# A fused retention and ELU feed-forward kernel: one weight part issued earlier, two FFN1 tiles in other PSUM banks, one weight transfer in place of two, and two units placed later

## The chip, the cores and the metric

The kernel runs on one core of a Trainium2 chip. Its time is the device time of an execution in microseconds (us), as the median of several runs. One execution was profiled; its trace has the start and the duration of each instruction on the engines: PE (TensorE, the matmuls, with PEld for its weight loads), DVE (VectorE), ACT (ScalarE), POOL (GpSimd) and SP (SyncE, which only issues transfers here). All places in time below are microseconds from the start of the profiled span.

## The reference

Retention (attention without softmax, with a decay by distance for each head) is followed by a feed-forward layer with an ELU between its two matmuls:

```python
batch, n_heads, seq, head_dim = (8, 8, 576, 64)      # q, k, v; float32
scores = (1 / sqrt(D)) * q @ k^T
gamma = 1 - 2 ** (-5 - arange(H))
Dmat = where(rel >= 0, gamma ** rel, 0)              # rel = row - column
attn = (scores * Dmat) @ v
x = attn.transpose(0, 2, 1, 3).reshape(4608, 512)
h = x @ w_in                                         # w_in 512 x 2048
g = where(h > 0, h, exp(min(h, 0)) - 1)
out = g @ w_out                                      # w_out 2048 x 512; float32
```

## The kernel before

**Units and groups.** The 4608 rows are cut into 36 units of 128 rows. Units come in groups (`GROUPS`): the first has units 0 to 2, then units 3, 4 and 5 stand alone, then groups of two, three and at last four units. A group's FFN1 has 16 tiles of 128 hidden columns; each tile is four matmuls over 128 x (128 times the group's units). `f1(g, n)` takes as many tiles at once as fill 512 columns of a bank: one for a group of three or four units, two for a group of two, four for a group of one.

**A unit's retention.** `scale_v` (POOL, L172) scales v by a decay factor for each key. `turn` (L180) transposes q and k on PE into a score tile in PSUM, and DVE copies one half out, then ACT the other (units from 12 on are transposed by a transfer instead). `scores` (L203) puts the products of keys and queries in PSUM, `masks` (DVE, L216) applies the causal mask, `inter` and `intra` (L227, L267) add what the carried state and the unit's own keys give, `state` and `state_out` (L243, L260) update the carried state, and `put_x` (DVE, L279) applies the decay for each query and writes the columns of `xt`, the input of FFN1. `product(u)` is `inter`, `state`, `intra`, `put_x` and `state_out` in a row. `stretch(u)` (L289) does the same for unit u, with the scores and masks of unit u + 1 around it.

**FFN1 and ELU.** `ffn1` (L336) issues the matmuls of a tile (`ph`), ACT takes the exponential (`e`, L354), POOL makes `m = e - 1` (L356), and DVE makes `g = min(max(ph, 0), m)` (L316), which is the ELU, since `m` is positive only where `ph` is. DVE's part is queued later than the others: `late` holds it until `tick` has been called three times (L318), and `finish(n)` (L312) queues what is n ticks old. `ffn1_part` (L324) issues the matmuls of a tile for some units only; `f1` then does the rest. `ffn2` and `ffn2_half` multiply g by w_out.

**PSUM.** FFN1 tiles use three `ps_h` banks (`h`) in turn and, where a tile is given the bank `m`, the single `ps_m` bank. The pool `ps_s` holds one tile of two banks, used by `turn` and `scores` one after the other. A bank is free for the next tile when its last reader is done; for an FFN1 tile this is DVE's g.

**The order of the work.** It is written out by hand up to FFN1 of group 2 (L419 to L512). In the first FFN1, tiles 0 to 3 are begun for units 0 and 1, `product(2)` is put between, and then all 16 tiles follow, with unit 3 among them: its turn after tile 5, its scores and `scale_v(3)` after tile 7, its product after tile 10. FFN1 of unit 3 follows, then halves of FFN2 of units 0 to 3. From there on a planner orders the work (L515 to L572): `slots` is the list of FFN1 and FFN2 pieces of PE, each of length about 1; `due` gives each unit a place in slots, interpolated between the starts of groups; `events` place the stretch of unit u at `due[u]`, `scale_v` of unit u + 2 at the same place, and the turn of unit u + 2 at a share of the way to the next unit. An event is queued ahead of the first slot whose middle lies at or past its place.

**Transfers.** POOL's queue issues the q and k loads and the weights, since these are cast to bf16 on the way. Weights come in parts: `load_w_in(n)` is a quarter of w_in, which serves tiles 4n to 4n + 3, and `load_w_out(c, f0, f1)` a piece of the column half c of w_out. v goes through SP's queue, except for unit 3. `load_v` with a second argument first lets that engine write one element of the buffer, which holds the transfer back until that engine gets there. POOL is in order: an issue stands in the same queue as `m` and `scale_v`.

Of the kernel before, what the change touches and what calls it, by code (L numbers as in the profile page):

```python
# [9 lines left out]
FP32 = mybir.dt.float32  # L10
BF16 = mybir.dt.bfloat16
I32 = mybir.dt.int32
AF = mybir.ActivationFunctionType
ALU = mybir.AluOpType
# [3 lines left out]
def kernel(  # L18
# [12 lines left out]
    B, H, S, D = q.shape  # L31
    DM, DF = moe_w_in.shape
    P = 128
    HP = H // 2
# [3 lines left out]
    R = 2 * S // P  # L38
# [9 lines left out]
    def place(u):  # L48

        pair, r = divmod(u, R)  # L50
        if r < 4:
            return [(0, 2 * pair, P * r, P)]
        if r == 4:
            return [(0, 2 * pair, 4 * P, 64), (64, 2 * pair + 1, 0, 64)]
        return [(0, 2 * pair + 1, 64 + P * (r - 5), P)]
# [6 lines left out]
    nat = ctx.enter_context(tc.tile_pool(name="nat", bufs=5))  # L62
# [9 lines left out]
    ps_s = ctx.enter_context(tc.tile_pool(name="ps_s", bufs=1, space=PSUM))  # L72
# [4 lines left out]
    raws, kns = {}, {}  # L77
# [10 lines left out]
    def load_qk(u, *cs):  # L88

        if u not in kns:  # L90
            kns[u] = qkpool.tile([P, 2, H, D], BF16, name="qkn", tag="qkn")
        for c in cs or (0, 1):
            for p0, b, s0, n in place(u):
                nc.gpsimd.dma_start(  # L94
                    kns[u][p0 : p0 + n, c], (q, k)[c][b, :, s0 : s0 + n, :].rearrange("h p d -> p h d")
                )
# [6 lines left out]
    def load_w_in(n):  # L103
        s = slice(n * 512, (n + 1) * 512)
        nc.gpsimd.dma_start(w_in_sb[:, :, s], w_in_v[:, :, s])

    def load_w_out(c, f0, f1):
        s = (slice(None), slice(f0, f1), slice(c * 256, c * 256 + 256))
        nc.gpsimd.dma_start(w_out_sb[s], w_out_v[s])
# [51 lines left out]
    gk = const.tile([P, R, H], FP32, name="gk")  # L161
# [7 lines left out]

    qkTs, vns, scs, pts, os_, sbs, sts = {}, {}, {}, {}, {}, {}, {}  # L170

    def scale_v(u):  # L172
        rv = raws[u]
        n = nat.tile([P, H, D], BF16, name="vn", tag="vn")
        nc.gpsimd.tensor_tensor(  # L175
            n, rv, gk[:, u % R].unsqueeze(2).to_broadcast([P, H, D]), ALU.mult
        )
        vns[u] = n

    def turn(u, bank=None, keys_on_v=False):  # L180

# [21 lines left out]
    def scores(u):  # L203
        t = qkTs[u]
        sc = ps_s.tile([P, 2, HP, P], FP32, name="sc", tag="sc")
        for hp in range(HP):
            for j in range(2):
                for i in range(2):
                    r = slice(i * D, (i + 1) * D)
                    nc.tensor.matmul(  # L210
                        sc[j * 64 : (j + 1) * 64, i, hp], t[r, 1, hp, j * 64 : (j + 1) * 64], t[r, 0, hp],
                        start=(hp == 0), stop=(hp == HP - 1), skip_group_check=True,
                    )
        scs[u] = sc

    def masks(u, i=None):  # L216

        if u not in pts:
            pts[u] = ppool.tile([P, 2, HP, P], BF16, name="pt", tag="pt")
        m = mask[:, 1 if u % R == 4 else 0]  # L220
        s = slice(0, 2) if i is None else slice(i, i + 1)
        nc.vector.tensor_tensor(  # L222
            pts[u][:, s].rearrange("p i h t -> p (i h) t"), scs[u][:, s].rearrange("p i h t -> p (i h) t"),
            m.unsqueeze(1).to_broadcast([P, (s.stop - s.start) * HP, P]), ALU.mult,
        )

    def inter(u):  # L227

        o = ps_o.tile([P, HP, P], FP32, name="o", tag="o")
        os_[u] = o  # L230
        r = u % R
        if r == 0:
            return
        n = 64 if r == 4 else P
        for hp in range(HP):
            for i in range(2):
                rows = slice(i * D, (i + 1) * D)
                nc.tensor.matmul(  # L238
                    o[rows, hp, :n], sbs[u][rows, hp], qkTs[u][rows, 0, hp, :n],
                    start=(hp == 0), stop=False, skip_group_check=True,  # L240
                )

    def state(u):  # L243

        r = u % R
        if r == 8:
            return
        if r in (0, 4):
            sts[0] = ps_st.tile([P, HP, D], FP32, name="st", tag="st")
        st = sts[0]  # L250
        rows = slice(64, P) if r == 4 else slice(0, P)
        for hp in range(HP):
            for i in range(2):
                h = 2 * hp + i
                nc.tensor.matmul(  # L255
                    st[i * D : (i + 1) * D, hp], kns[u][rows, 1, h], vns[u][rows, h],
                    start=(hp == 0 and r in (0, 4)), stop=(r in (3, 7)), skip_group_check=True,
                )
# [8 lines left out]
    def intra(u):  # L267
        o = os_[u]
        for hp in range(HP):
            for i in range(2):  # L270
                h = 2 * hp + i
                nc.tensor.matmul(  # L272
                    o[i * D : (i + 1) * D, hp], vns[u][:, h], pts[u][:, i, hp],
                    start=(u % R == 0 and hp == 0), stop=(hp == HP - 1), skip_group_check=True,
                )
# [3 lines left out]
    def put_x(u):  # L279
        g, i = group_of[u]  # L280
        if i == 0:
            xts[g] = xpool.tile([P, KJ, 512], BF16, name="xt", tag="xt")
        r = u % R
        s0 = P * r if r < 5 else 64 + P * (r - 5)
        nc.vector.tensor_tensor(  # L285
            xts[g][:, :, i * P : (i + 1) * P], os_[u], gx[:, :, s0 : s0 + P], ALU.mult
        )

    def stretch(u, ahead=True):  # L289

        ahead = ahead and u + 1 < NU
        if ahead:
            scores(u + 1)
        inter(u)
        state(u)
        intra(u)
        last = GROUPS[group_of[u][0]][-1] == u
        if last:
            put_x(u)
        if ahead:  # L300
            masks(u + 1)
        if not last:
            put_x(u)
        state_out(u)
# [7 lines left out]
    def finish(n=0):  # L312

        while late and late[0][0] <= slot[0] - n:
            _, gt_, ph, m, _ = late.pop(0)
            nc.vector.scalar_tensor_tensor(gt_, ph, 0.0, m, ALU.max, ALU.min)  # L316
# [5 lines left out]
    phs = {}  # L322

    def ffn1_part(g, ft, u0, u1, bank=None):  # L324

        pool, tag = bank or (ps_h, "ph")
        if (g, ft) not in phs:
            phs[g, ft] = pool.tile([P, 512], FP32, name="ph", tag=tag)
        c = slice(u0 * P, u1 * P)
        for j in range(KJ):  # L330
            nc.tensor.matmul(  # L331
                phs[g, ft][:, c], w_in_sb[:, j, ft * P : (ft + 1) * P], xts[g][:, j, c],
                start=(j == 0), stop=(j == KJ - 1), skip_group_check=True,
            )
# [74 lines left out]
    def product(u):  # L409
        inter(u)  # L410
        state(u)
        intra(u)
        put_x(u)
        state_out(u)

    h, m = (ps_h, "ph"), (ps_m, "pm")
# [7 lines left out]
    scale_v(0)  # L424
    load_w_in(1)
    scale_v(1)
    load_qk(3)
    load_v(3, queue=nc.gpsimd)
    scale_v(2)
    load_w_in(2)  # L430
    load_w_in(3)
    load_w_out(0, 0, 8)
    load_w_out(0, 8, 16)
    load_w_out(1, 0, 16)
    dummy(2)
    for u in range(2):
# [13 lines left out]
    def f1(g, n, bank=None):  # L450
        k = 512 // (P * len(GROUPS[g]))
        ffn1(g, k * n, bank)
# [4 lines left out]
    product(2)  # L457
    for n in range(2, 4):
        ffn1_part(0, n, 0, 2, m if n == 3 else None)
    for n in range(4):  # L460
        ffn1_part(0, n, 2, 3)
        f1(0, n)
    for n in range(4, 16):
        f1(0, n, m if n % 4 == 3 else None)
        if n == 5:
            turn(3)
        if n == 7:
            scores(3)
            masks(3, 0)
            scale_v(3)  # L470
        if n == 8:
            masks(3, 1)
        if n == 10:
            product(3)
    for n in range(4):
        f1(1, n, m if n == 3 else None)
        if n == 0:
            load_v(4, nc.vector)
        if n == 1:
            load_qk(4)  # L480
    finish()
    load_qk(5)
    load_v(5, nc.vector)
# [32 lines left out]
    for g in range(3, NG + 1):  # L516
# [10 lines left out]
        while a < len(f1s) or b < len(f2s):  # L527
# [4 lines left out]
                slots.append(f1s[a])  # L532
                a += 1
            now += slots[-1][3]
    due = {5: 0.0}
    last = 5
    for g in range(4, NG):
        u1 = GROUPS[g][-1]
# [3 lines left out]
    events = []  # L542
    for u in range(5, NU):
        def at(share):
            return due[u] + share * (due[u + 1] - due[u])
        events.append((due[u], 0, u))
        if u + 2 < PE_TURNED:
            events += [(due[u], 3, u + 2), (at(0.5), 1, u + 2)]
        if PE_TURNED <= u + 3 < NU:
            t = at(0.4) if u + 2 < PE_TURNED else due[u]  # L550
            events += [(t, 1, u + 3), (t, 3, u + 3)]
        if u + 5 < NU:
            events += [(at(0.25), 4, u + 5), (at(0.6), 5, u + 5)]
# [3 lines left out]
    for f, g, s, d in slots:  # L557
        while events and events[0][0] <= now + d / 2:
            _, kind, u = events.pop(0)
# [13 lines left out]
    u = NU - 1  # L573
# [31 lines left out]
```

## Time and profile before

| | us |
|---|---|
| median of 5 runs | 316.66 (316.49 to 317.78) |
| the profiled execution | 317.78 |
| its span, first to last instruction | 316.0 |
| PE busy in the span | 307.4 |
| PE busy in 0 to 20, of 20 | 16.89 |
| PE busy in 20 to 36, of 16 | 14.90 |
| PE busy in 36 to 56, of 20 | 19.48 |
| PE busy in 56 to 83, of 27 | 26.68 |
| PE busy in 120 to 280, of 160 | 159.86 |

The span is some 1.8 us shorter than the time of the execution that it was taken from, since the time also holds what lies before the first and after the last instruction. A row of a group of instructions gives its line, engine and operation, the tile written and the tiles read, the count, the busy time and the mean duration of one in nanoseconds, and then the idle time of the engine just ahead of them with what ended it. A row of the timeline gives start and duration, the engine and the line, and in brackets the idle time before it and what ended that. A row of the waits says who waited for whom: us in total, times, and the longest. PE's busy time counts each matmul to its modelled end, so a gap between two matmuls is longer in issue time than the idle time shown.

### The profile page before, as it was taken

The page shows a single profiled execution, that of the slowest core. Times are in us where ns is not written, and L with a number is a line of the kernel's source. Part 1 is how long each engine was busy: PE and PEld are TensorE (multiplying, and loading weights), DVE is VectorE, ACT ScalarE, POOL GpSimd, SP SyncE. Part 2 cuts the span into 40 slices and gives each one's busy share as a digit, 9 for nine tenths or more (in the row PEclk, how much of TensorE's full clock was granted, in tenths as well). Part 3 has the DMA queues.
Part 4 walks back from the last instruction along what each step waited for, and adds up shares of the span by engine and source line. Part 5 has one row for each costly group of instructions (what it writes and reads, how often), then busy time and mean ns, then how long its engine had stood idle before and what let it go on. Part 6 is the DMA issues. An engine that isn't in the chain of part 4 may idle for free.

```text
span 316.0 us, 7538 instructions
## 1 busy us (share of the span) xinstructions
PE 307.4 (97%) x3020; PEld 174.0 (55%) x3020; DVE 172.7 (55%) x279; ACT 131.1 (41%) x243; POOL 201.1 (64%) x288
## 2 busy tenths in 40 slices
PE   8789999999999999999999999999999999999995
PEld 3465888767766555555444444444444444444444
DVE  4458525667675666665665555555555555434300
ACT  6336323435534544344444444344444444344411
POOL 7967894887987787787777666766664433333300
PEclk9799999999999999999999999999999999999999
DMA  9999999995999999999999999999996200000111
GB/s 151 191 208 199 155 186 216 162 172 39 122 138 178 146 132 168 149 126 170 118 146 134 135 134 135 133 136 133 135 133 85 66 35 35 34 33 33 68 67 68
DMA packets 149235, 39.55 MB, mean 125 GB/s; under 512 B 137616, under 2 KB 145168, under 8 KB 149200
## 3 DMA queue, kind: packets, MB, share of 16 engines
q0 software_dynamic: 79264, 13.64, 56.0%
q1 hardware_dynamic: 67920, 23.14, 39.0%
q10 hardware_dynamic: 2016, 2.29, 2.3%
q8 instruction: 23, 0.38, 0.5%
q14 instruction: 12, 0.10, 0.1%
HBM read 36.70 MB, written 9.44 MB: 146 GB/s over the span
## 4 chain that ended last, share of the span: by engine, by line
PE 90%; DVE 3%; DMA 2%; POOL 2%; issue 1%; ACT 0%; POOLq 0%; DVEq 0%; ACTq 0%
PE ph L349 38%; PE pm L374 33%; PE pmh L390 5%; PE sc L210 4%; PE o L272 3%; PE st L255 2%; PE o L238 2%; DMA qkn<-in_k_dram 2%; PE tr L194 2%; DVE pt L222 1%; POOL qkn L94 1%; PE dum L407 1%; DVE g L316 1%; DVE xt L285 1%; PE ph L331 1%; POOL m L356 1%
## 5 line engine op out<-in xcount | busy, mean ns | idle before, releaser
L356 POOL TENSOR_SCALAR m<-e 128x512 bf16<-128x512 f32 (+1 forms) x156 | 91.0, 586 | 95.1 <-ACT e L354 90.3
L349 PE MATMUL ph<-xt,w_in_sb 128*128 128x512 bf16 (+3 forms) x816 | 143.2, 314 | 1.3 <-DVE g L316 1.1
L316 DVE SCALAR_TENSOR_TENSOR g<-ph,m 128x512 bf16<-128x512 f32 (+1 forms) x156 | 99.7, 648 | 80.7 <-POOL m L356 79.2
L354 ACT ACTIVATE e<-ph 128x512 f32<-128x512 f32 (+1 forms) x156 | 87.7, 565 | 125.0 <-PE ph L349 123.5
L374 PE MATMUL pm<-w_out_sb,g 128*128 128x512 bf16 x496 | 125.6, 379 | 0.0
L349 PEld LDWEIGHTS <-w_in_sb 128*128 128x128 bf16 x816 | 69.8, 98 | 54.8 <-issue 2.1
L374 PEld LDWEIGHTS <-g 128*128 128x128 bf16 x496 | 47.8, 98 | 53.2 <-issue 0.3
L222 DVE TENSOR_TENSOR pt<-sc,mask 128x1024 bf16<-128x1024 f32 (+1 forms) x37 | 44.1, 1193 | 19.0 <-PE sc L210 18.8
L175 POOL TENSOR_TENSOR vn<-rv,gk 128x512 bf16<-128x512 f32 x36 | 37.6, 1043 | 2.1 <-DMA rv<-in_v_dram 2.0
L94 POOL DMA_DIRECT2D qkn<-in_q_dram x39 | 35.1, 901 | 0.0
L94 POOL DMA_DIRECT2D qkn<-in_k_dram x39 | 33.4, 857 | 0.1
L285 DVE TENSOR_TENSOR xt<-o,gx 128x512 bf16<-128x512 f32 x36 | 24.7, 685 | 15.5 <-PE o L272 15.3
L381 ACT COPY ot<-pm 128x512 f32<-128x512 f32 x31 | 18.2, 586 | 14.5 <-PE pm L374 14.4
L264 ACT CAST sb<-st 128x256 bf16<-128x256 f32 x32 | 11.9, 372 | 19.2 <-PE st L255 16.4
L390 PE MATMUL pmh<-w_out_sb,g 128*128 128x256 bf16 (+1 forms) x176 | 18.5, 263 | 0.3 <-DVE g L316 0.3
L390 PEld LDWEIGHTS <-g 128*128 128x128 bf16 x176 | 15.7, 98 | 2.3 <-issue 0.5
L210 PEld LDWEIGHTS <-qkT 64*64 64x64 bf16 x576 | 9.4, 107 | 13.5 <-issue 11.2
L210 PE MATMUL sc<-qkT 64*64 64x128 bf16 x576 | 15.3, 224 | 0.3 <-DVE rv L83 0.2
L272 PE MATMUL o<-pt,vn 128*64 128x128 bf16 x288 | 14.3, 221 | 0.0
L238 PE MATMUL o<-qkT,sb 64*64 64x128 bf16 (+1 forms) x256 | 12.5, 217 | 0.0
L395 DVE COPY oth<-pmh 128x256 f32<-128x256 f32 (+1 forms) x6 | 2.4, 402 | 16.2 <-PE pmh L390 16.2
L196 ACT COPY qkT<-tr 128x512 bf16<-128x512 bf16 x12 | 7.0, 586 | 10.0 <-DVE qkT L195 3.9
(41 smaller groups left out, 93.2 us busy)
## 6 DMA issues: line engine op xcount, KB each, us to landing
rv<-in_v_dram SPq DMA_DIRECT2D x31, 256.0 KB, 5.3
out_dram<-ot SPq DMA_DIRECT2D x27, 256.0 KB, 2.4
qkn<-in_q_dram POOLq DMA_DIRECT2D x31, 128.0 KB, 5.3
qkn<-in_k_dram POOLq DMA_DIRECT2D x31, 128.0 KB, 5.7
w_in_sb<-in_moe_w_in_dram POOLq DMA_DIRECT2D x4, 512.0 KB, 10.0
out_dram<-oth ACTq DMA_DIRECT2D x9, 128.0 KB, 4.6
w_out_sb<-in_moe_w_out_dram POOLq DMA_DIRECT2D x2, 512.0 KB, 13.6
w_out_sb<-in_moe_w_out_dram POOLq DMA_DIRECT2D x1, 1024.0 KB, 18.2
```

Of the source, the lines that this page charges most:

```text
L94: nc.gpsimd.dma_start(kns[u][p0 : p0 + n, c], (q, k)[c][b, :, s0 : s0 + n, :].rearrange("h p d -> p h d"))
L175: nc.gpsimd.tensor_tensor(n, rv, gk[:, u % R].unsqueeze(2).to_broadcast([P, H, D]), ALU.mult)
L210: nc.tensor.matmul(sc[j * 64 : (j + 1) * 64, i, hp], t[r, 1, hp, j * 64 : (j + 1) * 64], t[r, 0, hp], start=(hp == 0), stop=(hp == HP - 1) ...
L222: nc.vector.tensor_tensor(pts[u][:, s].rearrange("p i h t -> p (i h) t"), scs[u][:, s].rearrange("p i h t -> p (i h) t"), m.unsqueeze(1).t ...
L272: nc.tensor.matmul(o[i * D : (i + 1) * D, hp], vns[u][:, h], pts[u][:, i, hp], start=(u % R == 0 and hp == 0), stop=(hp == HP - 1), skip_g ...
L285: nc.vector.tensor_tensor(xts[g][:, :, i * P : (i + 1) * P], os_[u], gx[:, :, s0 : s0 + P], ALU.mult)
L316: nc.vector.scalar_tensor_tensor(gt_, ph, 0.0, m, ALU.max, ALU.min)
L349: nc.tensor.matmul(ph[:, i * n : (i + 1) * n], w_in_sb[:, j, f : f + P], xts[g][:, j, :n], start=(j == 0), stop=(j == KJ - 1), skip_group_ ...
L354: nc.scalar.activation(e[:, w], ph[:, w], AF.Exp)
L356: nc.gpsimd.tensor_scalar(m[:, w], e[:, w], -1.0, 1.0, ALU.add, ALU.mult)
L374: nc.tensor.matmul(pm, gts[g, ft][:, it * P : (it + 1) * P], w_out_sb[:, ft], start=(ft == 0), stop=(ft == NFT - 1))
L390: nc.tensor.matmul(pm, gts[g, ft][:, it * P : (it + 1) * P], w_out_sb[:, ft, c0:c1], start=(ft == 0), stop=(ft == NFT - 1),)
```

## The change

Eight places change, in the order of the program:

- `scale_v` can do one half of the heads at a time.
- In `stretch(5)` alone, `finish(2)` queues the g that are two ticks old ahead of `put_x`.
- The third part of w_in is issued ahead of q, k and v of unit 3 instead of after `scale_v(2)`.
- The first column half of w_out is one transfer instead of two.
- FFN1 tiles 4 and 5 of the first group are put in the two banks of the score tile, and pieces of them are issued among the last pieces of tiles 0 to 3. The `m` bank is then used by the tiles whose number leaves 1 on division by 4, and by the second of the four tiles of unit 3 instead of the last.
- Unit 3: the turn after tile 9, `scale_v` in halves after tiles 9 and 10, scores after 11, product after 13.
- `load_qk(4)` is issued after all four tiles of FFN1 of unit 3 instead of after the second.
- Unit 5 is due at 0.6 slots instead of 0.0 (which moves unit 6 from 5.0 to 5.3), and the turns of units 7 and 9 come at 0.7 of the way instead of 0.5.

```diff
-    def scale_v(u):
-        rv = raws[u]
-        n = nat.tile([P, H, D], BF16, name="vn", tag="vn")
+    def scale_v(u, half=None):
+
+        if u not in vns:
+            vns[u] = nat.tile([P, H, D], BF16, name="vn", tag="vn")
+        h0, h1 = (0, H) if half is None else (half * HP, half * HP + HP)
         nc.gpsimd.tensor_tensor(
-            n, rv, gk[:, u % R].unsqueeze(2).to_broadcast([P, H, D]), ALU.mult
+            vns[u][:, h0:h1], raws[u][:, h0:h1],
+            gk[:, u % R, h0:h1].unsqueeze(2).to_broadcast([P, h1 - h0, D]), ALU.mult,
         )
-        vns[u] = n
...
         last = GROUPS[group_of[u][0]][-1] == u
+        if u == 5:
+            finish(2)
         if last:
             put_x(u)
...
     scale_v(1)
+    load_w_in(2)
     load_qk(3)
     load_v(3, queue=nc.gpsimd)
     scale_v(2)
-    load_w_in(2)
     load_w_in(3)
-    load_w_out(0, 0, 8)
-    load_w_out(0, 8, 16)
+    load_w_out(0, 0, 16)
     load_w_out(1, 0, 16)
...
+    two = ps_s.tile([P, 2, 512], FP32, name="ph2", tag="sc")
+    phs[0, 4], phs[0, 5] = two[:, 0], two[:, 1]
     for n in range(4):
         ffn1_part(0, n, 2, 3)
         f1(0, n)
+        if n in (1, 3):
+            ffn1_part(0, 4 + n // 2, 0, 2)
+    for n in (4, 5):
+        ffn1_part(0, n, 2, 3)
     for n in range(4, 16):
-        f1(0, n, m if n % 4 == 3 else None)
-        if n == 5:
+        f1(0, n, m if n % 4 == 1 else None)
+        if n == 9:
             turn(3)
-        if n == 7:
+        if n in (9, 10):
+            scale_v(3, n - 9)
+        if n == 11:
             scores(3)
             masks(3, 0)
-            scale_v(3)
-        if n == 8:
+        if n == 12:
             masks(3, 1)
-        if n == 10:
+        if n == 13:
             product(3)
     for n in range(4):
-        f1(1, n, m if n == 3 else None)
+        f1(1, n, m if n == 1 else None)
         if n == 0:
             load_v(4, nc.vector)
-        if n == 1:
-            load_qk(4)
+    load_qk(4)
     finish()
...
-    due = {5: 0.0}
+    due = {5: 0.6}
...
-            events += [(due[u], 3, u + 2), (at(0.5), 1, u + 2)]
+            events += [(due[u], 3, u + 2), (at(0.7 if u in (5, 7) else 0.5), 1, u + 2)]
```

## The prediction

> **What bounds the kernel now.** I read the page first: the busy shares, the slices and the chain that ended last. Then came the waits of TensorE (PE), the windows by stage, and the timeline of the stages that the change touches. All times are us from the span's start.
>
> ```profile
> PE 307.4 (97%) x3020; PEld 174.0 (55%) x3020; DVE 172.7 (55%) x279; ACT 131.1 (41%) x243; POOL 201.1 (64%) x288
> ...
> PEclk9799999999999999999999999999999999999999
> ...
> PE 90%; DVE 3%; DMA 2%; POOL 2%; issue 1%; ACT 0%; POOLq 0%; DVEq 0%; ACTq 0%
> ```
>
> PE is 97% busy and 90% of the chain, so an edit pays only where PE stands still. The windows (columns: length, then PE and PEld) say where that is: 1.1 us in 20 to 36, 0.5 in 36 to 56, nearly nothing later. The clock is full from 20 us, so filling a gap wins no clock.
>
> ```profile
> 20.00:36.00 16.00, 14.90 (x184) 10.87 (x182) 11.86 (x23) 10.58 (x22) 11.16 (x21) 1.00 1.35 199
> 36.00:56.00 20.00, 19.48 (x263) 16.87 (x265) 7.83 (x18) 5.16 (x12) 14.75 (x19) 1.00 1.48 179
> ...
> 120.00:200.00 80.00, 79.86 (x760) 40.36 (x759) 48.80 (x69) 33.98 (x64) 57.99 (x81) 1.00 1.20 143
> ```
>
> PE's waits after 12 us (us in total, times, longest) are four, and the change addresses all four. PE is counted busy until a matmul's modelled end, so I measure a gap from one start plus the issue time to the next start; that is larger.
>
> ```profile
> PE ph L349 <- DVE g L316: 1.1, 1, 1.1
> PE pmh L390 <- DVE g L316: 0.3, 1, 0.3
> PE sc L210 <- DVE rv L83: 0.2, 1, 0.2
> PE tr L194 <- DVE pt L222: 0.2, 1, 0.2
> ```
>
> **How the change is costed.** I lay out each engine's queue in its program order. An instruction starts when its engine is free and its inputs and its buffer are; a hand-over takes 0.05, a matmul's result 0.2 after its last issue. Durations are by form from the trace: 0.65 on PE for a 384-column FFN1 tile, 0.88 for a 512-column one, 0.45 for a turn, 0.35 for scores, 0.81 for unit 3's product; e, m and g 0.49, 0.51 and 0.55 at 384 columns (spaced 0.4, 0.48, 0.48 back to back), 0.60, 0.62 and 0.69 at 512. Applied to the kernel before, this puts tile 4 at 22.04 (trace 22.03) and the third half product at 39.08 (39.20), so I trust it for differences.
>
> ```profile
> L316 DVE SCALAR_TENSOR_TENSOR g<-ph,m 128x384 bf16<-128x384 f32 x16 | 8.5, 554 | 2.5 <-POOL m L356 1.9
> ...
> L356 POOL TENSOR_SCALAR m<-e 128x384 bf16<-128x384 f32 x16 | 8.0, 510 | 4.1 <-ACT e L354 3.6
> ```
>
> **Tiles 4 and 5 in the score banks.** Before, all four banks are taken by tiles 0 to 3, and tile 4 waits until g of tile 0 ends at 21.99: a gap from 20.75 to 22.03, 1.28. Now the four pieces of tiles 4 and 5 (two of 0.435, two of 0.22: 1.31) run there. They need w_in's second part, landed at 18.6, and masks(2), done at 17.7. Tile 6 starts at 22.12. From there no tile waits: 7 at 22.77, 8 at 23.42, 9 (in the pm bank, whose g of tile 3 ends at 23.9) at 24.08, turn(3) at 24.73 (g of tile 5 at 24.4), tile 12 at 26.84. **Minus 1.28.**
>
> **Unit 3 later.** The same instructions. Scores come two tiles behind the turn, as before. The halves of scale_v(3) cost POOL 0.55 each against 1.04 whole; they start at 25.9 and 27.4, and state(3) needs them at 28.5. g of tile 10 falls between the masks, so intra(3) waits 0.14; behind it stand tile 14 and all of PE. FFN1 of unit 3 then waits 0.10 for g of tile 12. The trace of before shows as much at its own product (27.47 to 27.59, and 0.09 in the tiles after it), so **nothing to plus 0.1**; FFN1 of unit 3 ends near 34.05 instead of 35.27.
>
> **load_qk(4) later.** Its four issues on POOL (34.98 to 37.77) stand ahead of the last two m, so g comes at 38.46 and PE stands from 38.74 to 39.20.
>
> ```profile
> 34.98 1.43 POOL L94 DMA_DIRECT2D qkn<-in_q_dram  x2
> 36.40 1.38 POOL L94 DMA_DIRECT2D qkn<-in_k_dram  x2
> 37.76 1.25 POOL L356 TENSOR_SCALAR m<-e 128x512 bf16<-128x512 f32 x2
> 38.46 1.29 DVE L316 SCALAR_TENSOR_TENSOR g<-ph,m 128x512 bf16<-128x512 f32 x2 [2.69 <-POOL m L356]
> ```
>
> After, the last g ends at 36.2 and is needed at 37.5: **minus 0.46**. The issues run from 35.45 to 38.25 and land 3.6 to 4.3 later, by 41.3; turn(4) needs them at 42.7. load_qk(5), scale_v(4) and load_qk(6) follow half a us or more earlier than now.
>
> **Transfers.** POOL's queue was q, k and v of unit 3, scale_v(2), w_in 2 and 3, three w_out. From issue plus time to landing they landed at 19.5, 20.3, 21.0, 23.4, 25.9, 28.7, 31.4 and 37.0, in order, with the DMA engines full. With w_in's third part first, its 0.80 issue delays q, k, v and scale_v(2) on POOL (to 15.3; product(2) needs it at 18.5). In the stream it takes 2.4 (21.0 to 23.4), so it lands at 21.1, and q, k, v of unit 3 at 21.9, 22.7, 23.4. Tile 8 needs it at 23.42: the old order would just have done. Turn(3) needs k at 24.73. Here a rule speaks against the change. The Trainium skill (DMA: Bandwidth & Descriptors, Anatomy of one DMA) puts a GpSimd DMA at about 2.0 us fixed plus bytes at 436 GB/s: by my estimate 4.4 us for the 1 MB read here, which puts k at 24.7, with no margin left. I take the landings, 2.4 and 2.5 apart, since the transfers overlap in the queue: 2 us of margin. The last w_in part lands at 25.9 as before, and tile 12 now needs it at 26.84, not 29.0: **0.9 left, the smallest margin of all.**
>
> ```profile
> 18.82 1.15 POOL L109 DMA_DIRECT2D w_out_sb<-in_moe_w_out_dram  x1 [1.06 <-DMA w_in_sb<-in_moe_w_in_dram]
> ```
>
> One transfer for half of w_out drops an issue (0.90 twice becomes about 1.15, by this row) and perhaps the 1.06 wait: the last w_out is the 14th transfer on POOL and waits for the 6th; now it is the 13th. If it is a limit on bytes in flight, the wait stays. POOL is free by 18.4 or 19.97; its first m comes at 20.88, so **nothing**. The same rule would save a fixed 2 us by merging; the trace's halves land 2.7 apart and the 1 MB transfer takes 5.6, so I save none. It lands at 31.4 (34.3 if I take the row's 18.2 from issue), and the first half product needs it at 34.05: 0 to 0.3.
>
> **Unit 5 later, turns at 0.7.** Before, scores(6) start at 55.83 for an end at 55.42 (0.41), turn(7) at 58.95 for 58.64 (0.31), turn(9) at 71.32 for 70.99 and stretched by 0.14 (0.47): 1.19.
>
> ```profile
> 54.73 0.42 DVE L195 COPY qkT<-tr 128x512 bf16<-128x512 bf16 x1 [1.10 <-PE tr L194]
> ...
> 55.08 0.68 DVE L316 SCALAR_TENSOR_TENSOR g<-ph,m 128x512 bf16<-128x512 f32 x1
> ...
> 55.83 0.42 PE L210 MATMUL sc<-qkT 64*64 64x128 bf16 x16 [0.24 <-DVE rv L83]
> ```
>
> These go, and three waits take their place. The planner's due times put unit 5 behind the fourth FFN1 tile of unit 4. That tile now comes 3.1 after the first and needs its bank; g of the first ends 3.47 after it (55.76, behind the turn's copy): 0.42 with the hand-over. Turn(7) moves from slot 2 to slot 4, unit 6's stretch stays at slot 5: one 0.88 tile between turn and scores(7) against a chain of 0.15 + 0.42 + 0.05 + 0.59 + 0.1 on DVE and ACT: 0.43. Turn(9) moves behind the second of four FFN1 tiles of group 4, and its copy now stands ahead of g of the first, whose bank the fourth needs: 0.42. f1(3,0) also waits 0.08 for put_x(5). New: 1.35. **Plus 0.15.** finish(2) puts g of that third tile ahead of put_x(5), done at 55.6, when put_x can start only at 55.9: nothing. Due times from unit 7 on are unchanged, and PE doesn't wait there.
>
> **Sum.** -1.28 + 0.1 - 0.46 + 0.15 = -1.49; the layout as a whole gives -1.46. The profiled execution (317.78, span 316.0 and 1.78 around it) would take 316.3. The five runs lie at 316.5 to 316.7 three times and at 317.7 to 317.8 twice, this one among them. Its clock digit 7 near 12 us and three dummies in 1.46 us, not 0.82, may be that difference; without it tile 12 comes 1.2 earlier and would wait about 0.3 for w_in, while POOL's freedom before 19.97 gives as much back. So I take 1.46 from the median: 316.66 - 1.46 = **315.2**.
>
> **Rivals.** 0.3%, 0.95 us, is about what tells a change from none.
> *The pipeline eats half.* DVE has 0.15 us of slack per tile, and masks, put_x and the turn's copy meet it between 25 and 30. If each of intra(3), tile 14 and f1(1,0) waits 0.3 more: 316.66 - 0.6 = 316.1, the same. For it: the layout's g end within 0.1 to 0.4 of their need.
> *The three new waits don't come*, because g is queued earlier than I think: 1.35 more, 313.9. Against it: the ordering of g behind two more tiles.
> *Slower: w_in's last part is late.* At tile 12 each us past 26.84 is a us of PE. The gain is gone at 28.3 and the kernel is 0.95 slower at 29.25, a landing 3.35 later than the stream's 25.9: 317.6. For it: the margin of 0.9. Against it: nothing is added ahead of it, and its issue stays at 15.3.
> *It doesn't do what it says:* the score tile hands over as one and tile 6 waits anyway: -0.46 + 0.25, 316.5.
>
> **Chances.** Forecast 0.50 (its own range 314.8 to 315.7), pipeline 0.25, no new waits 0.12, late w_in 0.10, no effect 0.03. Faster: 0.50 + 0.12 = 0.62. Same: 0.25 + 0.03 = 0.28. Slower: 0.10. The range leaves out the late part and the tail of the third: 314.1 to 316.6.
>
> **What would show it.** Right: no PE gap near 21; POOL's m of unit 3 ahead of four q and k issues; waits of 0.3 to 0.4 at the fourth FFN1 tile of unit 4, at scores(7) and at the fourth tile of group 4. Wrong: a wait on w_in_sb or qkn by PE between 23 and 27, or gaps of over 0.3 from 28 to 31.

## The result and the profile after

The changed kernel takes 315.62 us (median of 39 runs, 314.84 to 316.55); the kernel before took 316.68 (76 runs). The ratio is 0.9961, with a 95% interval of 0.9951 to 0.9970: 1.23 us faster, between 0.95 and 1.55. (The two medians are 1.06 apart.) The forecast was 315.2, a gain of 1.46, with a range of 314.1 to 316.6. The clock granted to PE is 0.995 or less on the mean in 22 of 104 executions of the kernel before (those run beside the experiments) and in 6 of 40 of the changed one, and the means of the others are 316.56 and 315.59, 0.97 apart.

The profiled execution after took 315.09 with a span of 313.3. First its waits of PE, all that the list has (us in total, times, longest):

```profile
PE tr L196 <- DMA qkn<-in_k_dram: 1.4, 2, 1.3
PE dum L411 <- DVE warm L120: 1.2, 1, 1.2
PE ph L353 <- DVE g L320: 0.2, 1, 0.2
PE sc L212 <- ACT qkT L198: 0.2, 1, 0.2
PE ph L353 <- DVE rv L83: 0.2, 1, 0.2
PE ph L353 <- DMA w_in_sb<-in_moe_w_in_dram: 0.2, 1, 0.2
PE tr L196 <- DMA qkn<-in_q_dram: 0.2, 1, 0.2
```

The 1.1 of PE on g and the 0.3 of the half product are gone. Three waits of 0.2 (on g, on qkT and on rv) stand in place of the old ones at scores(6) and turn(9), and one wait is new in kind: on w_in. The waits on k, on q and on `warm` lie in the first 13 us and are in the trace of before too. The windows say the same by stage (columns: length, PE busy, PEld, DVE, ACT, POOL, clock, DMA):

```profile
20.00:36.00 16.00, 15.78 (x193) 12.10 (x191) 13.30 (x27) 9.45 (x20) 12.64 (x24) 1.00 1.42 204
36.00:56.00 20.00, 19.78 (x292) 16.84 (x291) 8.40 (x18) 6.29 (x13) 15.40 (x20) 1.00 1.54 192
```

PE is busy for 15.78 of 16 where it was 14.90, and for 19.78 of 20 where it was 19.48. PE's timeline after, where the gap was:

```profile
17.57 3.26 PE L335 MATMUL ph<-xt,w_in_sb 128*128 128x256 bf16 x40
20.66 2.76 PE L353 MATMUL ph<-xt,w_in_sb 128*128 128x384 bf16 x16
...
25.74 1.47 PE L353 MATMUL ph<-xt,w_in_sb 128*128 128x384 bf16 x8 [0.22 <-DMA w_in_sb<-in_moe_w_in_dram]
...
27.96 5.05 PE L353 MATMUL ph<-xt,w_in_sb 128*128 128x384 bf16 x72
32.84 1.36 PE L394 MATMUL pmh<-w_out_sb,g 128*128 128x256 bf16 x11
```

The 40 matmuls of L335 are the old 24 and the 16 of tiles 4 and 5; tiles 6 to 9 (x16 at 20.66) follow without a break. The third line is tile 12, 0.29 late. And the three waits of the planner's part, each with the piece ahead of it:

```profile
51.67 1.06 PE L353 MATMUL ph<-xt,w_in_sb 128*128 128x128 bf16 x16
52.95 1.07 PE L353 MATMUL ph<-xt,w_in_sb 128*128 128x128 bf16 x16 [0.22 <-DVE rv L83]
...
58.07 1.06 PE L353 MATMUL ph<-xt,w_in_sb 128*128 128x128 bf16 x16
59.37 0.42 PE L212 MATMUL sc<-qkT 64*64 64x128 bf16 x16 [0.24 <-ACT qkT L198]
...
69.45 1.04 PE L353 MATMUL ph<-xt,w_in_sb 128*128 128x256 bf16 x8
70.73 1.05 PE L353 MATMUL ph<-xt,w_in_sb 128*128 128x256 bf16 x8 [0.24 <-DVE g L320]
```

From start to start less 0.88 for the piece, these are 0.40, 0.42 and 0.40; the prediction had 0.42, 0.43 and 0.42 at these very places. The first of them is listed under `rv`, because DVE writes one element of rv (L83) right behind the g that frees the bank, and both end near 52.9.

### The profile page after: what moved, and what is told of

It reads as the page before. It is cut to its first block, busy times and chain, and to the rows that moved or that the text cites. A ratio compares the mean times of both kernels' runs of the same rounds, so it can differ in the third digit from the quotient of the medians.

```text
span 313.3 us, 7555 instructions
## 1 busy us (share of the span) xinstructions
PE 305.6 (98%) x3028; PEld 173.8 (55%) x3028; DVE 172.5 (55%) x279; ACT 130.8 (42%) x243; POOL 200.7 (64%) x288
## 4 chain that ended last, share of the span: by engine, by line
PE 88%; DMA 6%; DVE 2%; POOL 2%; SPq 1%; issue 0%; ACT 0%; DVEq 0%
PE ph L353 37%; PE pm L378 34%; PE pmh L394 6%; DMA w_in_sb<-in_moe_w_in_dram 4%; PE sc L212 4%; PE o L274 3%; PE st L257 2%; PE o L240 2%; DMA rv<-in_v_dram 2%; PE tr L196 1%; DVE pt L224 1%; DVE g L320 1%; POOL vn L177 1%; POOL qkn L94 1%; DVE xt L287 0%; DVE qkT L197 0%
## 5 line engine op out<-in xcount | busy, mean ns | idle before, releaser
L353 PEld LDWEIGHTS <-w_in_sb 128*128 128x128 bf16 x808 | 68.9, 98 | 53.8 <-DVE g L320 0.9
L177 POOL TENSOR_TENSOR vn<-rv,gk 128x512 bf16<-128x512 f32 (+1 forms) x37 | 37.8, 1021 | 1.1 <-DMA rv<-in_v_dram 1.0
L287 DVE TENSOR_TENSOR xt<-o,gx 128x512 bf16<-128x512 f32 x36 | 24.7, 685 | 14.3 <-PE o L274 14.1
```

What stands on the lines that cost most here:

```text
L177: nc.gpsimd.tensor_tensor(vns[u][:, h0:h1], raws[u][:, h0:h1], gk[:, u % R, h0:h1].unsqueeze(2).to_broadcast([P, h1 - h0, D]), ALU.mult,)
L287: nc.vector.tensor_tensor(xts[g][:, :, i * P : (i + 1) * P], os_[u], gx[:, :, s0 : s0 + P], ALU.mult)
L353: nc.tensor.matmul(ph[:, i * n : (i + 1) * n], w_in_sb[:, j, f : f + P], xts[g][:, j, :n], start=(j == 0), stop=(j == KJ - 1), skip_group_ ...
```

## The experiments

In the trace after, PE has the full clock from the start and the first FFN1 piece begins at 15.79, not 17.21 as in the trace of before. The two traces are therefore not a clean pair, and the first run is a second trace of before. Each ratio below is to the kernel before as it was run beside that experiment (its medians there are 316.44 to 316.82), with its 95% interval; "the changed kernel" is 315.62 and 0.9961.

**before_again: the kernel before, once more.** No edit.

> The kernel before, unchanged, for a second trace of it. The trace shown of before has PE at a reduced clock near 12 to 14.5 us and takes 317.8; most of its runs take 316.2 to 316.9, and the trace after has the full clock there. Theory: with the full clock the first FFN1 piece starts near 15.8 instead of 17.2, the gap ahead of tile 4 is still 1.2 to 1.3 wide, and the time is 316.3. If POOL's last w_out issue (its end at 19.97 in the first trace) then holds up the first m, the gap is 1.5 to 1.7 wide instead. Rival: the difference of 1.2 us lies elsewhere, and the two traces agree until 20 us.

316.65, span 314.9, full clock. PE and POOL in its timeline:

```profile
17.52 1.94 PE L331 MATMUL ph<-xt,w_in_sb 128*128 128x256 bf16 x24
...
18.72 1.15 POOL L109 DMA_DIRECT2D w_out_sb<-in_moe_w_out_dram  x1 [1.43 <-DMA w_in_sb<-in_moe_w_in_dram]
...
19.89 1.94 POOL L356 TENSOR_SCALAR m<-e 128x384 bf16<-128x384 f32 x4
...
21.06 1.14 PE L349 MATMUL ph<-xt,w_in_sb 128*128 128x384 bf16 x6 [1.60 <-DVE g L316]
```

The first piece begins at 15.74, so the two traces now run alike until there. The 24 matmuls take 1.74 of issue and end at 19.26; tile 4 starts at 21.06. The gap is 1.80, not 1.28: POOL issues the last w_out until 19.87 and only then makes the first m. This is a clean pair, and PE in the changed kernel is ahead of it by 1.46 at the first half product (34.30 against 32.84), by 1.89 at the first FFN1 tile of unit 4 (51.32 against 49.43), and by 1.80 from scores(9) to the end (73.51 against 71.71, 307.92 against 306.12). The two spans are only 1.6 apart (314.9 and 313.3): behind the last issue of an output the trace after takes 0.2 longer.

**planner_undone.**

```diff
-        if u == 5:
-            finish(2)
...
-    due = {5: 0.6}
+    due = {5: 0.0}
...
-            events += [(due[u], 3, u + 2), (at(0.7 if u in (5, 7) else 0.5), 1, u + 2)]
+            events += [(due[u], 3, u + 2), (at(0.5), 1, u + 2)]
```

> The changed kernel with unit 5 due at 0.0, the turns of units 7 and 9 at 0.5, and no g queued ahead of put_x(5). Theory (three waits take the place of three): the waits at the fourth FFN1 tile of unit 4, at scores(7) and at the fourth tile of group 4 (0.40, 0.41, 0.41 in the trace after) go, those at scores(6), turn(7) and turn(9) come back (0.41, 0.31, 0.47); the layout gives 0.12 faster than the changed kernel: 315.5, at most 0.2 away from 315.6. Rival (the gain lies in the planner's part): 316.6 to 316.8.

315.39 (6 runs), 0.9957 (0.9940 to 0.9974). The waits at scores(6) and turn(9) are back, the three new ones are gone, and nothing is lost: the planner's part carries none of the gain, as far as an interval of 0.5 us to either side can tell. In this profile PE waits 0.9 for w_in at tile 12, not 0.2, though nothing differs up to there; that wait varies from run to run:

```profile
26.02 1.47 PE L351 MATMUL ph<-xt,w_in_sb 128*128 128x384 bf16 x8 [0.92 <-DMA w_in_sb<-in_moe_w_in_dram]
```

**w_in_old_place.**

```diff
-    load_w_in(2)
     load_qk(3)
     load_v(3, queue=nc.gpsimd)
     scale_v(2)
+    load_w_in(2)
     load_w_in(3)
```

> The changed kernel with the third w_in part issued after scale_v(2), as before. Theory: it lands near 23.0 to 23.4 instead of 20.7, and tile 8, due at 22.0, waits for it by 1.0 to 1.2; the 0.29 that tile 12 waits for the fourth part is then covered: 0.8 to 0.9 slower than the changed kernel, 316.4 to 316.5. Rival (the order of transfers hides nothing, since PE has slack there): 315.6, no wait of PE on w_in.

316.09 (22 runs), 0.9983 (0.9974 to 0.9993); against the changed kernel's interval this is slower, by about 0.7. PE's timeline at tile 8:

```profile
23.27 1.47 PE L353 MATMUL ph<-xt,w_in_sb 128*128 128x384 bf16 x8 [1.32 <-DMA w_in_sb<-in_moe_w_in_dram]
```

The wait is where it was expected, a little longer, and tile 12 no longer waits. The order of the transfers is worth about half of the gain, though it removes no wait that the kernel before had: it keeps the filled gap from turning up again at tile 8, two tiles after the filler.

**qk4_old_place.**

```diff
+        if n == 1:
+            load_qk(4)
-    load_qk(4)
     finish()
```

> The changed kernel with load_qk(4) after the second of the four FFN1 tiles of unit 3, as before. By the prediction's term alone: 0.46 slower, 316.1. By the layout of the changed kernel, where the third of these tiles holds the bank of the second half product instead of the third one: PE waits 2.1 at the second half product, 317.8. Rival (POOL's order does not reach PE here): 315.6.

319.64 (6 runs), 1.0089 (1.0066 to 1.0112): slower than either theory said. The wait is the 2.0 of the layout, at the second half product:

```profile
36.61 8.81 PE L394 MATMUL pmh<-w_out_sb,g 128*128 128x256 bf16 x64 [2.03 <-DVE g L320]
```

But these 64 matmuls take 8.81, where 64 at 0.108 are 6.9 and the result of the last one 0.2. The windows show why (seventh value after the length: the granted clock):

```profile
34.00:36.60 2.60, 0.58 (x6) 0.37 (x4) 0.73 (x2) 0.00 (x0) 2.60 (x5) 1.00 1.58 202
36.60:38.00 1.40, 1.39 (x9) 1.06 (x9) 0.90 (x3) 0.00 (x0) 1.40 (x2) 0.65 1.63 126
38.00:40.00 2.00, 2.00 (x11) 1.38 (x10) 0.00 (x0) 0.14 (x1) 1.45 (x3) 0.50 1.63 132
40.00:42.00 2.00, 2.00 (x19) 1.68 (x17) 0.03 (x1) 0.23 (x1) 1.87 (x3) 0.89 1.68 246
42.00:44.00 2.00, 2.00 (x21) 1.80 (x19) 0.40 (x2) 0.28 (x1) 1.39 (x2) 1.00 2.05 162
```

After the wait the clock is down to half and needs some 4 us to come back: 0.35 x 1.4 + 0.5 x 2 + 0.11 x 2 = 1.7 us more. The place of load_qk(4) belongs to the change of banks: with the second tile of unit 3 in `m`, its third tile holds the bank of the second half product.

**no_score_banks.**

```diff
-    two = ps_s.tile([P, 2, 512], FP32, name="ph2", tag="sc")
-    phs[0, 4], phs[0, 5] = two[:, 0], two[:, 1]
...
-        if n in (1, 3):
-            ffn1_part(0, 4 + n // 2, 0, 2)
-    for n in (4, 5):
-        ffn1_part(0, n, 2, 3)
```

> The changed kernel with FFN1 tiles 4 and 5 in the ps_h and ps_m banks in turn, issued whole after tile 3; everything else as changed. Theory: PE stands again for 1.2 to 1.3 ahead of tile 4, the 0.29 at tile 12 is covered by it, and behind it the layout has 0.14 more at unit 3's product: 1.07 slower than the changed kernel, 316.7. Rival (the gap only moves: what fills it is paid back by the pipeline of e, m and g before FFN1 of unit 3): 315.6 to 315.9.

316.81 (14 runs), 1.0005 (0.9987 to 1.0022): no gain is left. PE's timeline has a gap at tile 4 and another at tile 5, which now takes `m` and waits for g of tile 3:

```profile
20.48 0.81 PE L353 MATMUL ph<-xt,w_in_sb 128*128 128x384 bf16 x4 [1.10 <-DVE g L320]
21.91 3.44 PE L353 MATMUL ph<-xt,w_in_sb 128*128 128x384 bf16 x20 [0.62 <-DVE g L320]
```

The second gap, 0.78 from start to start (20.48 + 0.65 to 21.91), is not one of the kernel before, where tile 5 takes a `ps_h` bank and does not wait. It comes from the new use of `m`, so this run puts the share of the score banks too high, by up to these 0.78.

**w_out_two.**

```diff
-    load_w_out(0, 0, 16)
+    load_w_out(0, 0, 8)
+    load_w_out(0, 8, 16)
```

> The changed kernel with the first column half of w_out in two transfers, as before. Theory: POOL issues 0.6 longer and may wait for an earlier transfer, ending near 19.4 at the latest, within 0.1 of the first m (19.46 after): 0 to 0.1 slower, 315.6 to 315.7. Rival (POOL's wait holds up the first m and with it tile 6): 0.3 or more slower, 315.9 to 316.2, with the first m after 19.7.

315.99 (18 runs), 0.9972 (0.9959 to 0.9984): its interval overlaps that of the changed kernel, so the time doesn't decide. POOL waits again ahead of the last w_out (POOL's timeline, then the first m in the changed kernel):

```profile
18.57 1.15 POOL L109 DMA_DIRECT2D w_out_sb<-in_moe_w_out_dram  x1 [1.21 <-DMA w_in_sb<-in_moe_w_in_dram]
19.88 0.51 POOL L360 TENSOR_SCALAR m<-e 128x384 bf16<-128x384 f32 x1 [0.16 <-ACT e L358]
```

```profile
19.46 0.99 POOL L360 TENSOR_SCALAR m<-e 128x384 bf16<-128x384 f32 x2 [1.89 <-ACT e L358]
```

The first m starts after 19.7, which the rival named as its sign, but POOL is not what holds it up: it waits for e, and it starts 1.89 after the start of the 40 matmuls of L335 in both traces (17.99 to 19.88, 17.57 to 19.46). PE itself is 0.42 later in this execution, and it runs through from 17.99 to 23.69 without a wait. There is no room beyond that. In g_first_split_q4 below, where POOL has 14 transfers too, its last w_out ends at 19.82, the first m starts 2.08 after the start of the 40 matmuls, and tile 6 stands 0.16 (17.75 + 3.10 to 21.01):

```profile
17.75 3.26 PE L333 MATMUL ph<-xt,w_in_sb 128*128 128x256 bf16 x40
21.01 2.76 PE L351 MATMUL ph<-xt,w_in_sb 128*128 128x384 bf16 x16
...
19.83 1.00 POOL L358 TENSOR_SCALAR m<-e 128x384 bf16<-128x384 f32 x2
```

So in the changed kernel the single transfer is worth nothing in one trace and 0.16 in another. On the kernel before it should show more.

**before_w_out_one: the same edit alone, on the kernel before.**

```diff
-    load_w_out(0, 0, 8)
-    load_w_out(0, 8, 16)
+    load_w_out(0, 0, 16)
```

> The kernel before with the first column half of w_out in one transfer, and nothing else. Theory (the last w_out waits because it is the 14th transfer on POOL's queue, for the 6th, w_in's second part; and in executions with the full clock this holds up the first m, 19.89 instead of about 19.45, and with it tile 4): no wait of POOL, its issues end near 17.6 to 18.0, the gap ahead of tile 4 shrinks from 1.80 to 1.3: 0.4 to 0.5 faster than before, ratio near 0.9985. Rival (the wait is for bytes in flight, or it reaches no other engine): POOL's wait stays or the gap stays, and the time is that of before, 316.5.

316.49 (22 runs) against 316.82, 0.9990 (0.9974 to 1.0006): the size that was expected, but not clear of none. In the trace POOL has no such wait and the first m starts at 19.60. The 24 matmuls start at 17.71 and end at 19.45, and tile 4 starts at 20.75, so the gap is 1.30, where before_again has 1.80:

```profile
17.71 1.94 PE L331 MATMUL ph<-xt,w_in_sb 128*128 128x256 bf16 x24
20.75 1.46 PE L349 MATMUL ph<-xt,w_in_sb 128*128 128x384 bf16 x8 [1.10 <-DVE g L316]
```

The POOL wait follows the number of transfers, not their bytes, which are the same in all of these kernels: with 14 on POOL's queue up to the last w_out it is there, in all seven such traces (0.66 to 1.43; 1.06 and 1.43 in the two of before, 1.21 in w_out_two, 0.73 in w_in_split below), with 13 it is in none of seven (the changed kernel and before_w_out_one among them).

**g_first: what the new waits of the planner's part are for.**

```diff
-        if u == 5:
-            finish(2)
...
     f1(2, 1)
+    finish(2)
     turn(6)
...
-            events += [(due[u], 3, u + 2), (at(0.7 if u in (5, 7) else 0.5), 1, u + 2)]
+            events += [(due[u], 3, u + 2), (at(0.7 if u == 7 else 0.5), 1, u + 2)]
...
             elif kind == 1:
+                if u == 9:
+                    finish(2)
                 turn(u)
```

> The changed kernel with g of the first FFN1 tile of unit 4 queued on DVE ahead of the copy of turn(6), g of the first tile of group 4 ahead of the copy of turn(9), turn(7) at 0.5 of the way again, and no g queued ahead of put_x(5). Theory (the waits at the fourth tiles are for a g that stands behind a turn's copy): the waits of 0.40 and 0.41 at the fourth tiles shrink to 0.1, scores(6) and scores(9) wait 0.1, scores(7) do not wait but turn(7) does for 0.25: 0.7 faster than the changed kernel, 314.9. Rival (the bank is late for another reason, m or e): these waits stay, 315.6.

315.29 (12 runs), 0.9946 (0.9924 to 0.9969); the interval overlaps that of the changed kernel. DVE's timeline has the copy ahead of g in the changed kernel, and g ahead of the copy here:

```profile
51.87 0.43 DVE L197 COPY qkT<-tr 128x512 bf16<-128x512 bf16 x1 [1.10 <-PE tr L196]
52.21 1.30 DVE L320 SCALAR_TENSOR_TENSOR g<-ph,m 128x512 bf16<-128x512 f32 x2
```

```profile
52.71 0.69 DVE L318 SCALAR_TENSOR_TENSOR g<-ph,m 128x512 bf16<-128x512 f32 x1 [1.15 <-POOL m L358]
53.32 0.41 DVE L197 COPY qkT<-tr 128x512 bf16<-128x512 bf16 x1
```

The tile that waited 0.40 for its bank now follows the one ahead of it at once, and so does the fourth tile of group 4. So these waits were for a g behind a turn's copy. The time fell less than the 0.7 expected. This profile holds a wait that the trace after does not:

```profile
42.58 0.40 PE L196 MATMUL tr<-ident,qkn 128*128 128x128 bf16 x4 [0.65 <-DMA qkn<-in_k_dram]
```

Turn(4) waits for k of unit 4. Up to there g_first issues what the changed kernel issues, so this wait, too, comes in some executions and not in others.

**g_first_w_in_split and w_in_split: the fourth w_in part in two transfers,** on g_first and on the changed kernel.

```diff
-    def load_w_in(n):
-        s = slice(n * 512, (n + 1) * 512)
+    def load_w_in(n, c0=0, c1=512):
+        s = slice(n * 512 + c0, n * 512 + c1)
...
-    load_w_in(3)
+    load_w_in(3, 0, 256)
+    load_w_in(3, 256, 512)
```

> As g_first, and the fourth w_in part in two transfers of half the columns. Theory (the margin of 0.9 at tile 12 was the smallest, and it is gone where the clock is full from the start): the first half lands near 24.5, the 0.29 at tile 12 goes, unit 3's product waits 0.14 instead: 0.15 faster than g_first, 314.7. Rival (shorter rows take longer, or one more transfer on POOL's queue costs as much): not faster than g_first.

> The changed kernel with the fourth w_in part in two transfers of half the columns, and nothing else. Theory (of the 0.4 us that the forecast had too much, 0.3 stands at tile 12, which waits for this part in executions with the full clock): no wait of PE on w_in at tiles 12 to 15, 0.15 to 0.3 faster than the changed kernel, 315.3 to 315.5; POOL has 14 transfers again and waits ahead of the last w_out, without reaching the first m by more than 0.1. Rival (the 0.4 lies elsewhere, or two transfers cost what they save): 315.6 or more.

314.85 (7 runs), 0.9950 (0.9932 to 0.9968), and 315.16 (7 runs), 0.9943 (0.9923 to 0.9964). Neither trace has a wait on w_in. Both intervals overlap those of the kernels that they were built on: the medians are 0.44 and 0.46 lower, but the first ratio is no lower than that of g_first (0.9946), so a gain is not shown by the times. In w_in_split, turn(4) waits 0.81.

The landings of the k loads of unit 4 tell why turn(4) is at risk (issues in a short window; last value: median us from issue to landing). The kernel before:

```profile
qkn<-in_k_dram POOLq DMA_DIRECT2D x2, 64.0 KB, 3.6
```

The changed kernel, and then w_in_split:

```profile
qkn<-in_k_dram POOLq DMA_DIRECT2D x2, 64.0 KB, 4.6
```

```profile
qkn<-in_k_dram POOLq DMA_DIRECT2D x2, 64.0 KB, 6.1
```

In g_first it is 6.0, with the same issues up to there as in the changed kernel: the landing moves by 1.4 from one execution to another.

**g_first_split_q4 and g_first_split_v5: two ways to give turn(4) its margin back,** on g_first_w_in_split. The first issues one of the four transfers earlier:

```diff
+        if n == 2:
+            load_qk(4, 0, pieces=slice(0, 1))
-    load_qk(4)
+    load_qk(4, 0, pieces=slice(1, 2))
+    load_qk(4, 1)
```

> As g_first with w_in's fourth part split, and the first of the four transfers of load_qk(4) issued ahead of the last m of unit 3, where POOL has 0.27 to spare. Theory (k of unit 4 lands within 1 us of turn(4) and at times after it): the last of them is issued 0.4 earlier, turn(4) does not wait, no half product waits for g: 0.1 faster than the kernel without this step, 314.7 to 314.8. Rival (g of the last tile is now late for the third half product): 0.2 to 0.5 slower, 315.0 to 315.3.

315.19 (6 runs), 0.9942 (0.9922 to 0.9962): no gain over g_first_w_in_split can be told (a higher median, a lower ratio). The last k still lands 5.7 after its issue, turn(4) waits 0.17, and no half product waits for g. The second keeps v of unit 5 out of the way:

```diff
     load_qk(5)
-    load_v(5, nc.vector)
     scale_v(4)
...
         ffn2_half(u, 0, bank)
+        if u == 2:
+            load_v(5, nc.vector)
```

> As g_first with w_in's fourth part split, and load_v(5) held back until the third half product's copy, as late as before the change (there near 39, here near 38.4 instead of 34.8). Theory (k of unit 4 lands 4.6 to 6.1 after its issue instead of 3.6 to 3.8, because v of unit 5 now shares the DMA engines with it; that takes the margin at turn(4) and makes it wait 0.2 to 0.8 in three of the traces): the last k of unit 4 lands within 4.2 of its issue, turn(4) does not wait, scale_v(5) waits up to 1.5 on POOL where POOL has time: 314.5 to 314.7. Rival (the last w_out or the output transfers slow it): it still lands 4.6 to 6 after its issue and turn(4) waits at times: 314.9 to 315.2.

314.49 (6 runs, 313.96 to 315.76), 0.9942 (0.9922 to 0.9962). Past the first k load PE has no wait left in its list; this is the whole of it (the second row is the first dummy matmul of the program):

```profile
PE tr L196 <- DMA qkn<-in_k_dram: 1.5, 1, 1.5
PE dum L409 <- DVE warm L120: 1.2, 1, 1.2
```

The list leaves out waits below some 0.15: turn(7), back at 0.5 of the way, still starts 0.33 late here (56.24, for 55.03 + 0.88). The k loads land 4.7 to 4.9 after their issue: sooner than the 5.3 to 6.1 of the four variants before it, but not within the 4.2 that was expected, and no sooner than with v of unit 5 early in the changed kernel (4.6), planner_undone (4.7) and w_out_two (4.9). So it is not shown that v of unit 5 delays k. scale_v(5) waits 2.78 on POOL, more than expected, and PE doesn't feel it. Four of its six runs lie below the lowest of the changed kernel's 39 (314.84), so I take it for faster than the changed kernel, although the two intervals overlap; which of its three steps does it is open.

## Why the prediction was right, point by point

**Tiles 4 and 5.** Right, and the main thing: without it nothing is gained (no_score_banks). The size was 1.28 in the execution that it was read from and is 1.80 in before_again, since POOL's last w_out adds 0.5 there. The prediction named this for executions with the full clock and set it against 0.3 at tile 12; the clean pair has 0.5 against 0.29. So they are not even, as the prediction took them: the filled gap alone gains 0.2 more than the wait at tile 12 takes.

**Unit 3 later.** Right, by the traces alone (no run puts unit 3 back): read from start to start as in the prediction, 0.10 stands ahead of its product (25.74 + 1.30 to 27.14) and 0.06 in the tiles behind it, against 0.12 and 0.09 before.

**load_qk(4) later.** The 0.46 was right as a term (0.47 in before_again, 37.77 to 38.24, none after). The same step gave turn(4) a margin of 1.4, with landings 3.6 to 4.3 after the issue. That margin is the step that failed: the k loads land 4.2 to 6.1 after it in the kernels with the new order (4.6 in the changed kernel, 4.2 in w_in_old_place), and turn(4) waits 0.2 to 0.8 in three traces. Why they land later is open. v of unit 5, the last w_out and the outputs are in flight with them, but the run that holds v of unit 5 back doesn't set itself apart, and the others were not varied.

**Transfers.** The forecast landings 21.1, 21.9, 22.7, 23.4, 25.9 and 31.4 came out as 20.7, 21.7, 22.6, 23.4, 25.7 and 31.0. The rule of the Trainium skill (DMA: Bandwidth & Descriptors, Anatomy of one DMA), by which the prediction's estimate put k of unit 3 at 24.7, was not borne out: k landed at 22.6, and turn(3) ran at 23.26 without a wait. The margin at tile 12, called the smallest, is gone in executions with the full clock (0.29), and in planner_undone PE waits 0.9 there. A wait on w_in_sb between 23 and 27 was the prediction's own sign of being wrong; it came, too small to undo the gain. A margin read from one execution is good to about 1 us here. Merging the w_out transfers costs PE nothing, as said. What it gives was put at nothing, from an execution in which the first m was not held up; it is 0.5 in the kernel before at the full clock, and 0 and 0.16 in two traces of the changed one. That a count of transfers is behind POOL's wait was left open and is now shown.

**The planner's part.** Right in place and size: 1.22 of new waits for 1.19 of old ones, a loss of 0.09 on PE in the clean pair, and undoing it costs nothing that six runs can show.

**Sum.** PE gains 1.80 in the clean pair of traces (1.46 to the first half product, 0.43 at the half products, less 0.09), and the times of the two executions are 1.56 apart. The forecast says 1.46, and the runs say 1.23, with 1.46 inside the interval. At the full clock they say about 0.97 (0.8 to 1.15 by their scatter), and there 1.46 is too much. So the mechanism is right, and that the number fits is in part luck: the forecast took 0.5 of gap and 0.3 at tile 12 for even and turn(4) for safe, and a part of the 1.23 seems to come from a clock that is reduced less often and at less cost. What lies between the traces and the runs is most likely the waits for w_in at tile 12 and for k at turn(4), which come in some executions and not in others; the execution traced after is 0.5 faster than the mean of its kind. That they account for all of it is not shown.

## What to carry to other kernels

When a gap is filled, everything behind it comes earlier, and each transfer behind it loses that much margin: reckon the landings against the new times, and take a margin under 1 us for a wait that comes in part of the runs, as at tile 12 and turn(4) here. Two banks that lie idle for a few us are worth as much as the wait for a free one, if the pieces put there cover the latency of the first tile through its whole chain (e, m, g); here they cover it with less than 0.1 to spare. On an in-order engine, look at what an instruction that frees a bank is queued behind: g behind a copy costs the wait that moving the copy was to remove.

## What was not expected of the hardware

After a wait of PE of 2.0 us its clock fell to half: 0.50 from 38 to 40 us in qk4_old_place, and some 4 us until it was full again, so the wait cost 3.7 instead of 2.0. Five of the six runs of that kernel have a mean clock of 0.989 to 0.995. The sixth has 1.000 and takes 318.28, near the 317.8 of the layout, so with the same edit the clock does not always fall.

The length of one wait doesn't decide it. The trace of before has 0.50 from 12 to 15 us, after a wait of 1.39 for k; g_first_w_in_split has a wait of 1.63 at the same place and 1.00 from 12 to 15. First the wait and the window of before, then those of g_first_w_in_split (the granted clock is again the seventh value after the length):

```profile
10.25 0.40 PE L194 MATMUL tr<-ident,qkn 128*128 128x128 bf16 x4 [1.39 <-DMA qkn<-in_k_dram]
...
12.00:15.00 3.00, 3.00 (x33) 1.66 (x23) 1.65 (x2) 0.59 (x1) 3.00 (x4) 0.50 1.30 204
```

```profile
10.03 0.40 PE L196 MATMUL tr<-ident,qkn 128*128 128x128 bf16 x4 [1.63 <-DMA qkn<-in_k_dram]
...
12.00:15.00 3.00, 2.74 (x53) 1.68 (x53) 2.18 (x3) 0.96 (x2) 3.00 (x5) 1.00 1.25 206
```

The Trainium skill (TensorE: Matmul & The Clock Gate, Part 1) has the clock fall to half after an idle window of about 3.4 us; here it fell after waits of 2.0 and 1.39, and did not after others of 1.3 (w_in_old_place) and 1.63. What decides between them is open. To close a gap of 2 us was worth nearly twice its length in the trace of qk4_old_place; the gaps at tile 4 in the two traces of before, 1.28 and 1.80, left the clock at 1.00.
